# A recurrent-attention and Fourier-mixing kernel: another pairing and order of the last token tiles, and another list of steps

## The chip, the core and the metric

One core of a Trainium2 chip runs the whole program. The metric is device time in microseconds (us), the median of several executions. Engines: PE multiplies matrices, PEld is its weight load, DVE is the vector engine, ACT the scalar engine, POOL GpSimd, SP the sync engine, which here only issues DMAs. Each engine works through its own instructions in program order and waits on semaphores for the others.

## The reference

```python
# q, k, v, f_logit: (4 batches, 8 heads, 768 tokens, 48)
f = 1 / (1 + exp(-f_logit))
for t in range(768):
    state = f[t][:, None] * state + outer(k[t], v[t])
    y[t] = q[t] @ state
x = y, heads side by side                       # (4, 768, 384)
u = x + real(fft(fft(x, axis=1), axis=2))
un = (u - mean(u)) / sqrt(var(u) + 1e-6)        # over the 384 channels
out = u + maximum(un @ w_ch1, 0) @ w_ch2        # 384 -> 1536 -> 384
```

## The kernel before, in words

**Order by hand.** The program is written out by a list of words, ORDER (lines 27 to 48, 720 words). Each word runs one step of some generator, and every step appends its instructions to the queues of the engines it uses. So the list is the order on every engine, DMA issues on SP and POOL included. The tile framework adds the waits. The words:

- A number u (0 to 15): the next step of attention unit u, two heads of one batch (`attention`, `outputs`, `fold`). Batch b has the units 4b to 4b+3. The steps are: ACT Exp and Ln (L372, L373); DVE scan (L379, L380); ACT three Exp (L383 to L387); DVE two products (L391, L392); PE scores (L400); DVE masked copy (L404); PE first values and more scores, ACT copy `ao` (L559 to L579); PE other values and the state update `ds` (L559, L599); DVE state scan (L607); PE values from the state, ACT five copies (L616 to L629); PE transposes, ACT two copies (L636 to L641); DVE fold (L663 to L669); for the last two units of a batch one more fold (L678 to L687).
- K u: PE transposes the keys of unit u (L538) and ACT copies them to `kT` (L540), which `ds` reads.
- L u names: SP loads f, k, q or v of unit u (L206 to L213). r, R: SP fetches one or three of 24 raw 384 KB weight blocks into three buffers (L310). C: a block is turned into fp32 by ACT (L281), DVE (L283, L284) and POOL (L285); the first 12 blocks are `w1`, the other 12 `w2`.
- F b: a step of the Fourier stage of batch b: four of `z` (PE L725, ACT copies), then three of `mix` (PE L744, DVE sums, `moments`, `deviation`). H b: a step of `turns` (line 786), which normalizes a tile of 128 tokens (`moments`, `deviation`) or transposes it (`turn`, L780 to L784) for the products.
- P b: a step of `projected` (line 855): tiles of 128 tokens go in three pairs. For batch 0 the first layer is L872, and its first pair takes the plain second product `po` (L881, L885). For batches 1 to 3 the first layer is `hidden`, 15 steps a pair (L841 to L852), from sums of blocks. The second layer is seven products of quarter blocks, each 12 matmul records (L895), into two PSUM tiles `fx` (halves X, Y) and `fz` (halves V, Z); DVE makes sums for them (L902 to L913) and adds the results to the four half-rows c1, c2, d1, d2 of the pair's tiles c and d (L906 to L929), which `store` writes out.
- W, B: DVE makes the sums of weight blocks (L358 to L361, L813, L815). V, c: near the end weight blocks are read again and their smallest magnitude taken (L336, L344). M: `judge` (line 940) makes of these a flag, which every engine loads (line 1005) before a branch (line 1007) around a repair path that is not taken here.
- I, Z: POOL fills constants (`start`, with `bound`, which the first scan and the fillers read; `zeros`). D: eight filler matmuls on `bound` (L192). i, T, S: tables and the identity.

**Stores** (line 689). Tiles 1, 2, 3 and 5 go out by an indirect DMA from POOL, since their rows lie in another order; tiles 0 and 4 by plain DMAs from SP, tile 4 in three pieces (1, 15 and 112 rows); tile 0 of the last batch from ACT. All write the one output tensor, and the framework lets a store after an indirect one wait for its landing.

**The end.** The last batch's pairs are LAST_PAIRS = ((2, 5), (1, 4), (3, 0)). In the last pair tile 3 is c and tile 0 is d; product 7 into X ends it, and one DVE instruction (L929) adds X to both halves of tile 0's rows.

Of the kernel before, what the change touches and what calls it, by code (L numbers as in the profile page):

```python
# [10 lines left out]
ALU = mybir.AluOpType  # L11

C = 128
# [14 lines left out]
    "I L0f D L1f 0 D 0 1 L2f D D D D D L0q L0k D L1k 2 Z 0 D 1 i D D L1q L3q 0 0 0 L0v L3fk D 1 r 1 L2q D "  # L28
    "D L1v L2k 2 0 1 K0 3 0 0 D r 3 r D 2 0 1 1 2 C K1 L2v 1 2 1 C 3 2 C 1 K2 3 L4fk 4 2 r 1 2 L5fk D 4 5 "
    "L3v 1 3 2 D D T C 2 3 0 L4qv K3 5 3 0 2 3 D 3 2 3 S 2 3 D 3 L6fk 6 R 3 4 F0 5 F0 4 L5qv F0 C F0 5 "  # L30
    "L6qv K4 C r C 4 4 r F0 5 4 H0 H0 r C 4 H0 4 C L7fk r F0 r 7 F0 6 4 P0 C L7qv K5 P0 P0 r C r 5 C P0 r "
    "7 P0 5 6 4 6 P0 C C P0 5 K6 5 L8fk r C P0 7 7 P0 5 6 r P0 C 8 P0 r 6 r C P0 6 7 C K7 H0 C r 7 P0 r 6 "
    "C r 6 5 P0 C 6 H0 C P0 B 7 r C 6 r C 7 H0 L9fk L8qv P0 8 P0 P0 9 9 7 9 L9qv 6 P0 P0 P0 P0 9 7 9 K9 "
    "H0 P0 8 9 P0 P0 7 5 P0 P0 B P0 P0 8 7 B 9 8 4 9 H0 B W P0 P0 P0 9 P0 6 P0 P0 L11fk B P0 11 P0 P0 P0 "
    "P0 B B P0 11 9 8 K8 7 P0 P0 P0 11 8 F1 F1 F1 P0 P0 B L11qv F1 B P0 8 11 8 F1 11 8 L10fk P0 H1 B 10 B "
    "K11 P0 P0 P0 P0 L10qv 10 B 10 P0 10 P0 P0 10 H1 11 P0 P0 10 B B P0 B P0 H1 B P0 10 K10 P1 P1 P1 P1 "
    "P1 P1 P1 P1 L12fk P1 P1 P1 P1 P1 P1 F1 P1 F1 10 8 12 10 P1 8 12 10 12 9 P1 P1 P1 P1 L12qv 12 11 9 12 "
    "P1 H1 P1 H1 P1 12 11 K12 H1 H1 11 11 H1 L13fk P1 P1 P1 L13qv P1 P1 P1 P1 P1 P1 13 P1 P1 P1 P1 P1 13 "
    "P1 P1 12 10 P1 P1 13 13 12 10 12 11 P1 P1 P1 11 10 P1 L14fk 14 12 P1 K13 P1 11 F2 F2 P1 P1 14 P1 P1 "
    "L14qv P1 F2 P1 P1 14 P1 P1 P1 P1 P1 P1 14 F2 13 F2 P1 13 F2 P1 13 F2 P1 13 14 L15fk H2 15 13 14 13 "  # L40
    "K14 P1 15 L15qv 15 P1 P1 P1 14 15 H2 P1 H2 14 H2 P1 P2 14 P2 P2 P2 P2 P2 P2 P2 P2 P2 P2 P2 P2 P2 P2 "
    "13 14 15 K15 H2 H2 15 15 14 P2 V 15 H2 14 15 13 P2 14 c V 15 12 12 P2 P2 15 P2 15 V P2 P2 15 P2 F3 "
    "F3 F3 P2 H2 c V P2 P2 P2 V V P2 P2 P2 P2 P2 P2 P2 c P2 c c F3 P2 V F3 V F3 V c P2 P2 F3 P2 P2 P2 P2 "
    "P2 P2 H3 P2 H3 P2 V P2 P2 H3 P2 c P2 c c P2 P2 V P2 P2 P2 P2 P2 P2 P2 V P2 P2 P2 c c P2 c V V c V P2 "
    "V P2 P2 V P2 P2 H3 P3 c H3 P3 P3 P3 P3 P3 P3 P3 P3 P3 P3 P3 P3 c P2 P3 P3 H3 c P3 P3 P3 V P3 V P3 V "
    "c P3 P3 H3 P3 P3 H3 P3 c V P3 P3 P3 P3 P3 P3 P3 P3 V P3 P3 P3 P3 c P3 c P3 P3 P3 P3 P3 P3 P3 P3 P3 "
    "P3 V P3 c c P3 P3 P3 P3 P3 P3 c V P3 c P3 P3 P3 P3 P3 M P3 P3 P3 P3 P3 P3 P3 P3"
# [32 lines left out]
LAST_PAIRS = ((2, 5), (1, 4), (3, 0))  # L80
# [3 lines left out]
def kernel(  # L84
# [13 lines left out]
    nc = tc.nc  # L98
    B, HP, _, D, _, S = qkf.shape
# [589 lines left out]
    def store(b, c, rows):  # L689
# [7 lines left out]
        for i, j, o in {0: [(0, C, 0)], 4: [(0, 1, 3 * QS), (1, 16, HS + 1), (16, C, HS + 16)]}[c]:  # L697
            queue = nc.scalar if (b, c) == (B - 1, 0) else nc.sync
            queue.dma_start(out=out[b, o:o + j - i], in_=rows[i:j])
# [3 lines left out]
    def fnet(b, x):  # L703
# [52 lines left out]
        H1 = QD + 1  # L756
# [98 lines left out]
    def projected(b, x, again=False):  # L855
# [5 lines left out]
        for j, (c, d) in enumerate(PAIRS if b < B - 1 else LAST_PAIRS):  # L861
            if again:
                for _ in range((3, 3, 2)[j] if b < B - 1 else (3, 2, 3)[j]):
                    next(behind[b], None)
# [49 lines left out]
            yield  # L914
# [181 lines left out]
```

## Time and profile before

| | us |
|---|---|
| median of three runs (527.76 to 528.81) | 528.33 |
| the profiled execution | 527.43 |
| its span, first to last instruction | 525.7 |
| PE busy in it | 494.9 |
| DVE busy | 378.6 |
| ACT busy | 216.8 |

A profile is of one execution. The span lies within its time, with 1.75 us around it. Instructions are named by line, engine, operation and tiles (out<-in); "idle before" is the time in which the engine had nothing to run just ahead of one, and the name after it what ended that. A matmul's end is modelled, so PE can look full where it is only nearly so. PEclk is the clock that the chip granted to PE, in tenths.

The costliest groups (busy us, mean ns, idle before):

```profile
L850 DVE TENSOR_TENSOR h<-h,ub 128x512 f32<-128x512 f32 x81 | 55.6, 688 | 38.9 <-PE ub L841 27.2
L872 PE MATMUL up<-unT,w 128*128 128x256 f32 x216 | 50.0, 382 | 0.0
L841 PE MATMUL ub<-wide,w 128*128 128x128 f32 x360 | 45.2, 277 | 2.1 <-DVE wide L815 2.1
L895 PE MATMUL fx<-block,h 128*128 128x192 f32 x264 | 46.8, 327 | 0.0
L379 DVE TENSOR_TENSOR_SCAN W<-g,bound 112x768 f32<-112x768 f32 x12 | 21.2, 1766 | 8.7 <-ACT g L373 8.7
```

### The profile page before, as it was taken

What the parts mean: (1) busy time and instruction counts of PE and PEld (TensorE: products, weight loads), DVE (VectorE), ACT (ScalarE), POOL (GpSimd) and SP (SyncE); (2) the same over time, 40 slices, a digit from 0 to 9 for tenths busy, and PEclk for the clock granted to TensorE, in tenths of its full rate; (3) what the DMA queues carried; (4) which work ended last, traced back from release to release, by engine and by line L of the source; (5) the groups of instructions that cost most, each with busy time, mean ns of one, the idle gap of its engine ahead of it and who ended that gap; (6) DMA issues with size and microseconds to landing.
All of it is one profiled execution on the core that took longest, in us unless ns stands there. A gap on an engine that the chain in (4) does not pass through costs nothing.

```text
span 525.7 us, 13813 instructions
## 1 busy us (share of the span) xinstructions
PE 494.9 (94%) x5854; PEld 452.8 (86%) x5854; DVE 378.6 (72%) x746; ACT 216.8 (41%) x520; POOL 61.3 (12%) x85
## 2 busy tenths in 40 slices
PE   6788699989999999999999999999999999999994
PEld 5676478756898889999999999998999999999994
DVE  4669999868986378588688696679586665565571
ACT  7484658753423351452543524341431404131220
POOL 3047034541002000000001000000001000010000
PEclk9879799999999999999999999999999999999998
DMA  8979476672002110222112012122140330410201
GB/s 222 277 192 268 98 198 187 184 215 85 28 28 85 54 56 28 57 55 86 54 56 84 1 55 73 46 62 68 53 122 15 107 135 1 136 61 1 92 2 36
DMA packets 20505, 48.15 MB, mean 92 GB/s; under 512 B 3409, under 2 KB 6034, under 8 KB 20434
## 3 DMA queue, kind: packets, MB, share of 16 engines
q1 hardware_dynamic: 19186, 43.43, 29.3%
q0 software_dynamic: 1104, 3.54, 1.8%
q8 instruction: 48, 0.79, 0.6%
q14 instruction: 23, 0.19, 0.1%
q10 hardware_dynamic: 144, 0.20, 0.1%
HBM read 42.44 MB, written 4.72 MB: 90 GB/s over the span
## 4 chain that ended last, share of the span: by engine, by line
PE 80%; DVE 9%; DMA 4%; issue 2%; ACT 2%; SPq 0%; POOL 0%; DVEq 0%; POOLq 0%; ACTq 0%
PE ub L841 23%; PE fx L895 16%; PE fz L895 12%; PE up L872 6%; PE z L725 4%; PE mix L744 3%; PE y L559 3%; PE po L881 2%; PE sc L400 2%; PE y L616 2%; DMA raw<-in_w_ch_dram 2%; PE pt L783 2%; PE ds L599 1%; PE st L538 1%; DVE W L379 1%
## 5 line engine op out<-in xcount | busy, mean ns | idle before, releaser
L850 DVE TENSOR_TENSOR h<-h,ub 128x512 f32<-128x512 f32 x81 | 55.6, 688 | 38.9 <-PE ub L841 27.2
L692 POOL DMA_INDIRECT out_dram<-x,place x16 | 17.7, 1107 | 383.7 <-DVE x L925 254.0
L848 ACT ACTIVATE h<-ub 128x512 f32<-128x512 f32 x54 | 32.0, 593 | 45.0 <-PE ub L841 45.0
L872 PE MATMUL up<-unT,w 128*128 128x256 f32 x216 | 50.0, 382 | 0.0
L841 PE MATMUL ub<-wide,w 128*128 128x128 f32 x360 | 45.2, 277 | 2.1 <-DVE wide L815 2.1
L895 PE MATMUL fx<-block,h 128*128 128x192 f32 x264 | 46.8, 327 | 0.0
L895 PE MATMUL fx<-w,h 128*128 128x192 f32 x264 | 45.6, 327 | 0.0
L872 PEld LDWEIGHTS up<-unT,w 128*128 128x128 f32 x216 | 39.8, 190 | 6.2 <-ACT h L874 0.9
L841 PEld LDWEIGHTS ub<-wide,w 128*128 128x128 f32 x360 | 42.4, 192 | 3.1 <-PE fx L895 1.2
L895 PEld LDWEIGHTS fx<-block,h 128*128 128x128 f32 x264 | 43.3, 190 | 0.4 <-DVE x L922 0.2
L852 ACT ACTIVATE h<-h 128x512 f32<-128x512 f32 x45 | 28.3, 630 | 36.9 <-DVE h L850 36.8
L895 PEld LDWEIGHTS fx<-w,h 128*128 128x128 f32 x264 | 42.8, 190 | 0.4 <-issue 0.2
L841 PE MATMUL ub<-unT,w 128*128 128x128 f32 x288 | 36.8, 275 | 0.0
L285 POOL TENSOR_TENSOR w<-w,raw 128x384 uint32<-128x384 uint32 x24 | 28.1, 1173 | 71.6 <-ACT raw L281 42.8
L841 PEld LDWEIGHTS ub<-unT,w 128*128 128x128 f32 x288 | 34.5, 192 | 0.1
L784 ACT COPY unT<-pt 128x384 f32<-128x384 f32 x24 | 11.4, 485 | 48.5 <-PE pt L783 48.5
L841 PE MATMUL ub<-unT,wide 128*128 128x128 f32 x216 | 29.1, 278 | 0.0
L841 PE MATMUL ub<-wide 128*128 128x128 f32 x216 | 28.6, 275 | 0.4 <-DVE wide L815 0.4
L379 DVE TENSOR_TENSOR_SCAN W<-g,bound 112x768 f32<-112x768 f32 x12 | 21.2, 1766 | 8.7 <-ACT g L373 8.7
L874 ACT ACTIVATE h<-up 128x256 f32<-128x256 f32 x36 | 13.8, 386 | 31.7 <-PE up L872 31.4
L841 PEld LDWEIGHTS ub<-unT,wide 128*128 128x128 f32 x216 | 26.4, 192 | 0.5
L841 PEld LDWEIGHTS ub<-wide 128*128 128x128 f32 x216 | 26.3, 192 | 0.5 <-PE ub L841 0.5
(189 smaller groups left out, 1001.6 us busy)
## 6 DMA issues: line engine op xcount, KB each, us to landing
raw<-in_w_ch_dram SPq DMA_DIRECT2D x24, 384.0 KB, 5.3
v<-in_v_dram SPq DMA_DIRECT2D x16, 288.0 KB
k<-in_w_ch_dram SPq DMA_DIRECT2D x12, 384.0 KB
g<-in_w_ch_dram SPq DMA_DIRECT2D x12, 384.0 KB, 3.5
k<-in_qkf_dram SPq DMA_DIRECT2D x14, 288.0 KB, 5.9
g<-in_qkf_dram SPq DMA_DIRECT2D x12, 288.0 KB, 5.6
q<-in_qkf_dram SPq DMA_DIRECT2D x12, 288.0 KB, 4.9
wide<-in_qkf_dram SPq DMA_DIRECT2D x10, 288.0 KB, 5.2
```

Of the source, the lines that this page charges most:

```text
L285: nc.gpsimd.tensor_tensor(bits, bits, lo, ALU.add)
L379: nc.vector.tensor_tensor_scan(W, g, bound[:R], 0.0, ALU.add, ALU.min)
L559: nc.tensor.matmul(y[FILL[g], c // 3, c % 3 * C + t.start:c % 3 * C + t.stop], lhsT=vals[rows, o:o + (64 if g == 0 else D)], rhs=weights, ...
L692: nc.gpsimd.indirect_dma_start(out=out.rearrange("b s d -> (b s) d"), out_offset=bass.IndirectOffsetOnAxis(ap=place[:, b, i:i + 1], axis=0 ...
L725: nc.tensor.matmul(z[:, cols], lhsT=src[:, j, lo:hi], rhs=tab[:, t, T % 2, cols], start=(i == 0), stop=(i == len(parts) - 1), skip_group_c ...
L744: nc.tensor.matmul(mix[:, o], lhsT=zz[:rows_of[T], T, PLACES[c]], rhs=cd[:rows_of[T], T, :NQ - odd], start=(i == 0), stop=(i == 1))
L841: nc.tensor.matmul(chains[chain][:, m * 128:(m + 1) * 128], lhsT=block(w)[:, m * 128:(m + 1) * 128], rhs=tokens(a), start=(new and m == 0) ...
L848: nc.scalar.activation(out, got, kind, scale=1.0 if how == "=+" else -1.0)
L850: nc.vector.tensor_tensor(out, out, got, ALU.add if how == "+" else ALU.subtract)
L852: nc.scalar.activation(out, out, AF.Relu)
L872: nc.tensor.matmul(pp[:, :256], lhsT=w1[:, kt, m * 128:(m + 1) * 128], rhs=unT[:, kt], start=(kt == 0), stop=(kt == 2))
L895: nc.tensor.matmul(out, lhsT=h[:, m], rhs=blocks[i][:, m], start=(start and m == 0), stop=(m == H - 1), skip_group_check=True)
```

## The change

Three things change. The list has the same 720 words in another order. LAST_PAIRS becomes ((2, 5), (1, 3), (0, 4)), and `turns` follows it. For the pair (0, 4) the products come in the order 1, 2, 4, 6, 5, 7, 3, so that the last one adds to c2 alone, the second half of tile 0's rows; tile 4 is complete one product earlier and is stored then; tile 0 goes out in two halves of 192 columns, both from SP.

```diff
@@ -25,26 +25,26 @@
 
 
 ORDER = (
-    "I L0f D L1f 0 D 0 1 L2f D D D D D L0q L0k D L1k 2 Z 0 D 1 i D D L1q L3q 0 0 0 L0v L3fk D 1 r 1 L2q D "
-    "D L1v L2k 2 0 1 K0 3 0 0 D r 3 r D 2 0 1 1 2 C K1 L2v 1 2 1 C 3 2 C 1 K2 3 L4fk 4 2 r 1 2 L5fk D 4 5 "
-    "L3v 1 3 2 D D T C 2 3 0 L4qv K3 5 3 0 2 3 D 3 2 3 S 2 3 D 3 L6fk 6 R 3 4 F0 5 F0 4 L5qv F0 C F0 5 "
-    "L6qv K4 C r C 4 4 r F0 5 4 H0 H0 r C 4 H0 4 C L7fk r F0 r 7 F0 6 4 P0 C L7qv K5 P0 P0 r C r 5 C P0 r "
-    "7 P0 5 6 4 6 P0 C C P0 5 K6 5 L8fk r C P0 7 7 P0 5 6 r P0 C 8 P0 r 6 r C P0 6 7 C K7 H0 C r 7 P0 r 6 "
-    "C r 6 5 P0 C 6 H0 C P0 B 7 r C 6 r C 7 H0 L9fk L8qv P0 8 P0 P0 9 9 7 9 L9qv 6 P0 P0 P0 P0 9 7 9 K9 "
-    "H0 P0 8 9 P0 P0 7 5 P0 P0 B P0 P0 8 7 B 9 8 4 9 H0 B W P0 P0 P0 9 P0 6 P0 P0 L11fk B P0 11 P0 P0 P0 "
-    "P0 B B P0 11 9 8 K8 7 P0 P0 P0 11 8 F1 F1 F1 P0 P0 B L11qv F1 B P0 8 11 8 F1 11 8 L10fk P0 H1 B 10 B "
-    "K11 P0 P0 P0 P0 L10qv 10 B 10 P0 10 P0 P0 10 H1 11 P0 P0 10 B B P0 B P0 H1 B P0 10 K10 P1 P1 P1 P1 "
-    "P1 P1 P1 P1 L12fk P1 P1 P1 P1 P1 P1 F1 P1 F1 10 8 12 10 P1 8 12 10 12 9 P1 P1 P1 P1 L12qv 12 11 9 12 "
-    "P1 H1 P1 H1 P1 12 11 K12 H1 H1 11 11 H1 L13fk P1 P1 P1 L13qv P1 P1 P1 P1 P1 P1 13 P1 P1 P1 P1 P1 13 "
-    "P1 P1 12 10 P1 P1 13 13 12 10 12 11 P1 P1 P1 11 10 P1 L14fk 14 12 P1 K13 P1 11 F2 F2 P1 P1 14 P1 P1 "
-    "L14qv P1 F2 P1 P1 14 P1 P1 P1 P1 P1 P1 14 F2 13 F2 P1 13 F2 P1 13 F2 P1 13 14 L15fk H2 15 13 14 13 "
-    "K14 P1 15 L15qv 15 P1 P1 P1 14 15 H2 P1 H2 14 H2 P1 P2 14 P2 P2 P2 P2 P2 P2 P2 P2 P2 P2 P2 P2 P2 P2 "
-    "13 14 15 K15 H2 H2 15 15 14 P2 V 15 H2 14 15 13 P2 14 c V 15 12 12 P2 P2 15 P2 15 V P2 P2 15 P2 F3 "
-    "F3 F3 P2 H2 c V P2 P2 P2 V V P2 P2 P2 P2 P2 P2 P2 c P2 c c F3 P2 V F3 V F3 V c P2 P2 F3 P2 P2 P2 P2 "
-    "P2 P2 H3 P2 H3 P2 V P2 P2 H3 P2 c P2 c c P2 P2 V P2 P2 P2 P2 P2 P2 P2 V P2 P2 P2 c c P2 c V V c V P2 "
-    "V P2 P2 V P2 P2 H3 P3 c H3 P3 P3 P3 P3 P3 P3 P3 P3 P3 P3 P3 P3 c P2 P3 P3 H3 c P3 P3 P3 V P3 V P3 V "
-    "c P3 P3 H3 P3 P3 H3 P3 c V P3 P3 P3 P3 P3 P3 P3 P3 V P3 P3 P3 P3 c P3 c P3 P3 P3 P3 P3 P3 P3 P3 P3 "
-    "P3 V P3 c c P3 P3 P3 P3 P3 P3 c V P3 c P3 P3 P3 P3 P3 M P3 P3 P3 P3 P3 P3 P3 P3"
+    "L0f Z I 0 L0q L2q D D L1f L0k D 0 D 0 i D 1 L2f 2 0 D D D L0v 0 L1k K0 D 0 0 D L1q 0 1 D r 1 L3fk D "
+    "D D L1v 2 0 L2k 1 D r r D 1 2 1 3 3 0 C K1 1 2 0 C 1 L3q 2 1 3 C L2v 2 r K2 L4fk 3 L3v L5fk 1 2 1 D "
+    "T 2 0 4 3 D C S 1 2 5 3 D 2 3 2 4 K3 3 D L5qv L4qv 5 4 3 2 3 L6fk 3 2 3 5 R 3 F0 F0 4 6 F0 L6qv F0 C "
+    "C 4 C 5 4 F0 r 5 K4 D 4 H0 r 4 r H0 C H0 4 C r L7fk F0 6 4 P0 C P0 6 5 P0 7 C F0 4 P0 r K5 r C L7qv "
+    "P0 P0 r r 5 6 C 6 5 r 7 C 5 P0 r 7 P0 C P0 5 r 7 K6 C P0 6 C P0 r r 6 7 7 C C 6 6 r 5 P0 P0 r C 6 r "
+    "C K7 H0 r P0 C 7 L9fk 6 H0 L8fk P0 L8qv C B 7 C H0 B 7 B 9 9 B 8 P0 8 9 P0 P0 L9qv P0 6 8 P0 P0 P0 "
+    "P0 9 P0 P0 8 7 B 9 K9 P0 P0 5 P0 B 6 P0 P0 B P0 7 W P0 9 B H0 9 8 9 B H0 7 P0 L11fk P0 11 P0 P0 P0 "
+    "P0 P0 P0 4 11 9 P0 P0 P0 P0 P0 9 B P0 P0 P0 P0 7 L11qv P0 8 11 F1 P0 8 K8 F1 F1 11 F1 L10fk 8 8 10 "
+    "F1 P0 8 11 H1 L10qv B 10 F1 P0 B P0 B P0 11 P0 P0 10 B 10 H1 P0 10 K10 P0 B 10 H1 10 K11 L12fk P1 P1 "
+    "P1 P1 P1 P1 P1 B P1 P1 P1 P1 P0 P1 P1 P1 F1 P1 P1 H1 10 9 12 10 P1 P1 12 10 9 8 P1 P1 P1 L12qv 12 11 "
+    "12 12 8 11 P1 L13fk 12 11 H1 10 H1 P1 11 H1 H1 P1 P1 P1 P1 P1 P1 P1 P1 P1 P1 P1 P1 P1 P1 10 P1 P1 12 "
+    "K12 10 P1 12 L13qv 11 P1 L14fk 12 11 P1 13 13 12 P1 P1 11 P1 14 13 P1 F2 P1 14 F2 P1 P1 P1 P1 P1 P1 "
+    "P1 P1 P1 P1 P1 14 P1 13 F2 P1 L14qv 14 P1 F2 13 13 F2 13 K13 F2 14 13 H2 F2 13 14 H2 P1 L15fk P1 P1 "
+    "15 15 13 K14 P1 P1 L15qv P1 14 P1 H2 14 H2 H2 P2 14 P2 P2 15 P2 P2 P1 P2 P2 P2 15 V P2 P2 P2 P2 P2 "
+    "P2 P2 13 14 15 H2 H2 15 K15 15 13 12 15 14 P2 15 14 15 P2 P2 V c 12 P2 15 P2 c V 14 P2 15 P2 H2 P2 "
+    "P2 P2 15 c F3 F3 F3 P2 V V P2 P2 P2 c V c P2 V P2 c P2 P2 V P2 F3 c P2 P2 V F3 F3 P2 F3 H3 P2 P2 P2 "
+    "P2 P2 P2 P2 P2 H3 P2 V P2 P2 V H3 P2 P2 c P2 P2 V P2 c c P2 P2 P2 V P2 P2 P2 P2 P2 P2 P2 c P2 P2 V "
+    "P2 H3 V P2 P2 H3 P3 H3 c P3 P3 c P3 P3 c P3 P3 P3 P3 c V P3 V P2 P3 P3 P3 c P3 P3 P3 P3 P3 V V P3 P3 "
+    "P3 P3 V H3 P3 P3 P3 H3 P3 c P3 P3 P3 P3 c P3 P3 P3 P3 P3 V P3 P3 P3 P3 P3 P3 P3 P3 c P3 P3 P3 P3 P3 "
+    "V P3 P3 c P3 V P3 c P3 c P3 P3 V c c P3 P3 P3 P3 P3 P3 M P3 P3 P3 P3 P3 P3 P3 P3"
 )
 
 
@@ -77,7 +77,7 @@
 FLIP = 1
 
 PAIRS = ((0, 3), (2, 5), (1, 4))
-LAST_PAIRS = ((2, 5), (1, 4), (3, 0))
+LAST_PAIRS = ((2, 5), (1, 3), (0, 4))
 
 
 @with_exitstack
@@ -695,8 +695,7 @@
                 in_=rows, in_offset=None)
             return
         for i, j, o in {0: [(0, C, 0)], 4: [(0, 1, 3 * QS), (1, 16, HS + 1), (16, C, HS + 16)]}[c]:
-            queue = nc.scalar if (b, c) == (B - 1, 0) else nc.sync
-            queue.dma_start(out=out[b, o:o + j - i], in_=rows[i:j])
+            nc.sync.dma_start(out=out[b, o:o + j - i], in_=rows[i:j])
 
     behind, turned_of = {}, {}
 
@@ -785,7 +784,7 @@
 
         def turns():
 
-            for step in ((0, [3], 3, [4, 5], 2, 5, 1, 4) if b < B - 1 else ([4, 5], 2, 5, 1, 4, [3], 3, 0)):
+            for step in ((0, [3], 3, [4, 5], 2, 5, 1, 4) if b < B - 1 else ([4, 5], 2, 5, [3], 1, 3, 0, 4)):
                 if isinstance(step, list):
                     for c in step:
                         moments(c)
@@ -860,7 +859,7 @@
         tt = nc.vector.tensor_tensor
         for j, (c, d) in enumerate(PAIRS if b < B - 1 else LAST_PAIRS):
             if again:
-                for _ in range((3, 3, 2)[j] if b < B - 1 else (3, 2, 3)[j]):
+                for _ in range((3, 3, 2)[j]):
                     next(behind[b], None)
             unT = turned_of[b][j].rearrange("p k t n -> p k (t n)")
             h = ph1.tile([128, NF, 2, 128], F32, tag="h1", name=f"h1_{b}_{j}")
@@ -912,6 +911,26 @@
             tt(c1, Y, c1, ALU.add)
             tt(h12, h12, h11, ALU.subtract)
             yield
+            both = x[:, d].rearrange("p (a n) -> p a n", a=2)
+            if (b, c) == (B - 1, 0):
+                nc.sync.dma_start(out=out[b, :C, :HD], in_=c1)
+                product(6, X, h11)
+                tt(d1, V, d1, ALU.add)
+                yield
+                product(5, Z, s1)
+                tt(c2, X, c2, ALU.add)
+                yield
+                product(7, X, h21)
+                tt(d2, Z, d2, ALU.add)
+                yield
+                product(3, Z, h12)
+                tt(both, X.unsqueeze(1).to_broadcast([128, 2, HD]), both, ALU.add)
+                store(b, d, x[:, d])
+                yield
+                tt(c2, Z, c2, ALU.add)
+                nc.sync.dma_start(out=out[b, :C, HD:], in_=c2)
+                yield
+                continue
             product(5, Z, s1)
             tt(d1, V, d1, ALU.add)
             yield
@@ -925,7 +944,6 @@
             tt(c2, Z, c2, ALU.add)
             store(b, c, x[:, c])
             yield
-            both = x[:, d].rearrange("p (a n) -> p a n", a=2)
             tt(both, X.unsqueeze(1).to_broadcast([128, 2, HD]), both, ALU.add)
             store(b, d, x[:, d])
             yield
```

## The prediction

> **What bounds the kernel now.** I read the page's totals and its slices first, then stretches of 25 us.
>
> ```profile
> span 525.7 us, 13813 instructions
> PE 494.9 (94%) x5854; PEld 452.8 (86%) x5854; DVE 378.6 (72%) x746; ACT 216.8 (41%) x520; POOL 61.3 (12%) x85
> PEclk9879799999999999999999999999999999999998
> ```
>
> PE at 94% looks like the bound of everything, but the slices differ. The table of stretches (PE, PEld, DVE, ACT, POOL busy, then granted clock, DMA share, GB/s) shows where:
>
> ```profile
> 0.00:25.00 25.00, 16.90 (x352) 15.61 (x352) 13.67 (x15) 15.07 (x24) 4.78 (x29) 0.93 0.96 244
> 25.00:50.00 25.00, 21.62 (x566) 18.17 (x566) 20.48 (x36) 15.71 (x40) 12.65 (x17) 0.86 0.86 223
> 50.00:75.00 25.00, 18.23 (x305) 14.35 (x306) 23.35 (x51) 15.25 (x43) 7.05 (x8) 0.86 0.60 162
> 75.00:100.00 25.00, 25.00 (x347) 20.88 (x348) 24.22 (x38) 19.79 (x50) 10.71 (x8) 1.00 0.68 186
> 100.00:125.00 25.00, 23.09 (x337) 15.54 (x328) 18.32 (x32) 13.19 (x31) 8.39 (x8) 1.00 0.64 188
> 125.00:150.00 25.00, 25.00 (x335) 21.64 (x334) 22.32 (x42) 11.24 (x29) 1.51 (x1) 1.00 0.12 37
> ```
>
> From 25 to 100 us DVE is full and PE is not; from 125 on PE is full. So the head of the list is a DVE stage, the rest a PE stage. The DVE's waits up to 60 us and the chain around 110 us say how the first ends:
>
> ```profile
> DVE stt L607 <- PE ds L599: 7.0, 2, 3.8
> DVE W L379 <- ACT g L373: 6.3, 1, 6.3
> DVE at L404 <- PE sc L400: 1.2, 1, 1.2
> ```
>
> ```profile
> 109.37 5.48 DMA raw<-in_w_ch_dram
> 114.85 0.02 issue
> 114.87 0.37 DVE w L283
> ```
>
> DVE loses 6.34 us to the first load and its Exp and Ln, 1.20 to unit 0's scores and 7.0 to the state scans of units 0 and 1 (3.25 at 18.4, 3.77 at 28.0), 14.8 with a gap of 0.2. From 31.8 to 102 it has no gap over 0.3 us. Then the last raw weight blocks pace it (a block is fetched when the third one before it has left POOL), until block 24 is converted and PE runs on at 116.8. After that PE's waits over 0.3 us sum to 3.7 us in 400.
>
> Tail: the last product ends at 518.85, and then
>
> ```profile
> 518.88 0.56 DVE L929 TENSOR_TENSOR x<-fx,x 128x384 f32<-128x384 f32 x1 [1.59 <-PE fx L895]
> 520.42 0.38 ACTq L699 DMA_DIRECT2D out_dram<-x  x1
> ```
>
> ACT issues 0.98 us after DVE has finished: its wait (504.22 to 520.38) ends with the landing of tile 3's indirect store (last at 520.35). The store lands at 523.60, SP then walks its closing waits from 523.61 to 524.87, and the span ends at 525.66: 6.81 us after PE.
>
> **The last pair.** It has the same seven products (1.95 us each) in another order, so PE is unchanged. Product 6 comes 1.95 us earlier: it needs h11, which L907 finished at 510.35, where PE would load for it at 510.72, so 0.37 us of cover. Product 3 is last and only a 128x192 add follows: 0.36 (rows L922, L925) in place of 0.56. Tile 3's indirect store is now in the middle pair, some 28 us earlier, so nothing is left to wait for. Tile 4's three stores come into this pair on SP: L699 issued such three from 490.60 to 491.70, 1.1 us, and they fall under product 3 (1.95 us from its predecessor's end, less 0.6 for the add). With that cover gone, the last store is up to 1.1 later. Where they stood before, two rereads (L336, issued 491.74 and 492.21) were queued behind them on SP; those are freed, and the flag they feed was ready at 505.5, 13 us early, so that is worth nothing. Counting from PE's end: add done 0.40, SP issues 0.45 to 0.82, landing about 2.6 (L699's median is 2.0 from issue). That would save 2 us. But SP also has its flag load and its branch behind that store. Before, they ran at 505.51 to 506.42 (0.91), and the next SP event came at 509.09, 2.67 later, hidden under products. Now they lie on the path: 0.82 + 0.05 + 0.91 + 2.67 = 4.45, and 0.18 for two waits that SP had passed before: 4.63 against 4.76. **Tail: -0.1**; bounds -2.0 (the 2.67 hidden after all) and +1.1 (PE's own branch took 3.79).
>
> [...]
>
> LAST_PAIRS and the turns move one moments step (0.73 DVE, 0.5 ACT) from before the third pair's turns to before the second's, under some 330 us of PE-bound time already past: 0, at worst the 0.7 itself. The counts (3, 2, 3) belong to the branch that is not taken.
>
> **The head of the list.** Every word occurs as often as before (720 words), so only order counts. Up to the first F0 both lists hold the same DVE work: four units, four weight blocks, the scans of units 4 and 5, 45.0 us by the means of the rows (per unit scan 1.94, L391 and L392 1.91, L404 1.03, L607 0.75, fold 2.46; L283 and L284 1.15 per block; 4.2 for the two later folds); up to block 24 both hold 95.5. So DVE's lead is its idle time alone, and I replay the new order with row durations:
> - Z ahead of I puts 2.54 us of POOL (3.29 to 5.83 before) ahead of `bound`: ready at 4.4, not 1.9. Fillers start later; the first scan, at 6.34, keeps 1.9 of cover.
> - DVE: scan 0 from 6.34 to 8.3, as before. ACT now does unit 0's Exp (0.84) next, ahead of units 1 and 2: DVE waits 0.9 and multiplies from 9.2 to 11.1 (before: to 12.4).
> - PE scores to 12.2 (DVE waits 1.1), copy to 13.2, scan 1 to 15.1, scan 2 to 17.05.
> - ACT: unit 0 to 10.5, Exp and Ln of unit 1 to 12.3, of unit 2 to 14.2, kT (K0, moved up) to 14.85, ao to 15.35. PE's values and ds (0.85 + 0.8) end at 17.0: the state scan waits for nothing, where it waited 3.25.
> - State scan to 17.8, unit 1's products to 19.7. PE has six fillers (0.67 each) after ds, to 21.0, and scores to 22.0: DVE waits 2.3.
> - Then scan 3, C, unit 2's products and C lead to unit 1's state scan at 29.2; its ds is there at 27.4. Cover 1.8 where 3.77 was lost.
>
> Idle 6.34 + 0.9 + 1.1 + 2.3 = 10.6 against 14.8, so **4.2 us** of lead. PE had two waits put to "issue" here, 1.15 at 17.4 and 2.26 at 22.7, which I cannot place in the new order; I take off half of the smaller: **-3.6**. Bounds: -4.5 and, if the two together fall on DVE's path, -0.8.
>
> Does the lead reach PE? Take, for each PE step that needs a DVE step, the DVE work ahead of and with the one less the PE work ahead of the other. Its largest value is 8.7 before (unit 5's copy, 69.8 against 61.1) and 8.6 after (unit 6's products, 72.8 against 64.2); the largest sets how late PE is for a given DVE. So PE follows by the same 3.6. The weight blocks: 12, 15, 18, 21 and 24 were begun at 83.9, 92.5, 99.6, 106.7 and 114.9; their places in DVE work are the same within 2 us, and L8fk no longer stands between the fetches (it was issued at 87.9 to 90.6, ahead of a fetch at 91.5). Three blocks in 7.5 us from a start 3.6 earlier: block 24 at 111.3, -3.6 again. Its adds then find po done, so the 2.58 us that DVE waited at L885 may shrink; that is DVE's, not the path's.
>
> **The rest of the list** reorders PE steps whose sum is the same. Unit 12's scores stand straight after their DVE products (1.07 us of PE work between them before), while units 8, 9 and 11 gain such cover. Bounds: all 3.7 us of PE's waits gone, or as much again; nearest to the equal sum of covers, I take +0.2.
>
> Sum on the profiled run (527.43, that is the span and 1.75 around it): -0.1 - 3.6 + 0.2 = -3.5, so 523.9. The median of the three is 0.90 above it: **524.8**, own range 522.5 to 527.0.
>
> **Rivals.**
> 1. *More.* PE's waits at issue fall where DVE does not care (-0.6 more), the branch's fetch overlaps (-1.0) and the block waits shrink by half (-1.7): 521.5. For it: 102 to 117 is paced by fetches, and L8fk leaves them. Against: the fetch cycle of 7.5 us is buffers, not traffic.
> 2. *One state scan waits again.* Unit 3's stands right behind K3 and its values; by the replay its ds comes 0.4 us before DVE wants it. One wait of the old size (3.25 to 3.77) gives the lead back: 524.8 + 3.5 = 528.3, no change.
> 3. *Slower: unit 0's v is late.* q0 and q2 now go ahead of f1 and f2, with DMA engines 96% busy. Ahead of and with v0 stand 2.56 MB (six loads of about 0.34, ident, v): at the 222 GB/s of the first slice it lands at 12.3, at the 98 of the worst slice near 27. PE waits for it in order, the state scan with it, and DVE stands behind the scan. Later than 13.2 it costs what it is late; from 17.4 the lead is gone; from 18.5 the kernel is measurably slower; at 19.5 it is +2.1 net: 530.4. For it: no landing of v is listed. Against: k and q land in 5 to 6 us, and v0 is issued three microseconds earlier than it was.
>
> **Chances.** The forecast 0.50, rival 1 0.16, rival 2 0.14, rival 3 0.20. A difference of 0.2% (1.06 us) is about what this measurement tells from none. Faster: 0.50 (less 0.015), 0.16, and a quarter of rival 2: 0.68; slower: rival 3 and a little of rival 2: 0.21; same: 0.11. The range holds rival 1's near half and rival 3 up to 530: 521.0 to 530.0.
>
> **What would show it.** DVE's first waits: 0.9, 1.1 and 2.3 in place of 1.2, 3.25 and 3.77; the first z of batch 0 near 54 (57.6 before); block 24 begun near 111.3; PE's last end near 515.4; SP's last store 0.45 after it and SP's first closing wait 3.6 after that store's issue has ended. Wrong would be: a state scan that waits 3 us again, v0 landing after 13.2, or PE's waits after 125 us growing past 4 us.

## The result

| | before | after |
|---|---|---|
| median of 20 runs, us | 528.32 (527.42 to 531.83) | 525.92 (523.41 to 529.41) |
| ratio after to before | | 0.9957, 95% interval 0.9940 to 0.9974 |
| the profiled execution | 527.43 | 527.98 |
| its span | 525.7 | 526.3 |

The change saves 2.4 us in the median. The execution that was profiled with the result is one of the long ones of its kernel: it is longer than the profiled one of before, though the median is shorter. So the changed kernel was profiled a second time (called "the second execution" below: 524.12 us, span 522.3). The two traces of one program, side by side, show what an execution can do to the head of the list.

From the page of the first execution: span, busy engines, and the granted clock in 40 slices.

```profile
span 526.3 us, 13807 instructions
PE 494.9 (94%) x5854; PEld 453.4 (86%) x5854; DVE 378.3 (72%) x746; ACT 218.4 (42%) x520; POOL 58.8 (11%) x85
PEclk9789699999999999999999999999999999999998
```

Its stretches (PE, PEld, DVE, ACT, POOL busy, then granted clock, DMA share, GB/s):

```profile
0.00:25.00 25.00, 16.14 (x301) 14.90 (x301) 11.13 (x12) 15.28 (x24) 4.80 (x29) 0.86 0.96 249
25.00:50.00 25.00, 19.93 (x558) 16.76 (x561) 23.31 (x37) 15.33 (x40) 10.07 (x11) 0.86 0.66 169
50.00:75.00 25.00, 18.93 (x341) 14.26 (x333) 21.19 (x48) 13.98 (x40) 6.26 (x13) 0.80 0.67 181
100.00:125.00 25.00, 23.74 (x372) 16.60 (x371) 21.80 (x35) 16.27 (x35) 9.53 (x9) 1.00 0.69 196
```

PE's busy time is 494.9 in both kernels, whose matmuls (5854) are the same. In the first 25 us DVE did less than before (11.13 against 13.67), at a granted clock of 0.86 against 0.93; between 100 and 125 it did more (21.80 against 18.32), because its waits for the raw blocks have shrunk (from 98 to 125 us: 1.7 in place of 3.7) and its wait of 2.6 for `po` is gone. The same stretches of the second execution:

```profile
0.00:25.00 25.00, 16.38 (x366) 14.89 (x367) 13.50 (x14) 15.39 (x24) 4.82 (x29) 1.00 0.94 242
100.00:125.00 25.00, 24.65 (x238) 16.58 (x239) 23.13 (x41) 16.17 (x34) 7.52 (x7) 1.00 0.72 204
```

DVE's waits up to 60 us (total, times, longest), first execution and then the second:

```profile
DVE W L379 <- ACT g L373: 6.5, 1, 6.5
DVE at L404 <- PE sc L400: 4.3, 2, 3.1
DVE stt L607 <- PE ds L599: 4.2, 2, 2.8
```

```profile
DVE at L404 <- PE sc L400: 2.4, 2, 1.2
DVE stt L607 <- PE ds L599: 4.0, 3, 1.5
```

The state scans (L607) waited 7.0 us before; they still wait 4.2 and 4.0. The scores (L404) waited 1.2 before and now 4.3 or 2.4, because the second unit's scores have six fillers ahead of them.

The chain around 110 us, first execution and then the second:

```profile
112.18 4.41 DMA raw<-in_w_ch_dram
116.58 0.02 issue
116.61 0.37 DVE w L283
```

```profile
108.34 3.60 DMA raw<-in_w_ch_dram
111.94 0.02 issue
111.97 0.95 DVE w L283
```

Block 24 is converted at 116.6 and 112.0 (114.9 before). PE's last matmul ends at 519.43 and 515.32 (518.84 before). The distance between these two marks is 402.8, 403.4 and 404.0: **what happens ahead of block 24 arrives at the end nearly undiminished, and what lies behind it differs by 1.1 us between these three traces.** Between the two executions of the changed kernel block 24 differs by 4.6 us and the rest by 0.5, so this spread is made in the first 115 us. In the fourteen traces of this study that distance lies between 402.8 and 405.5.

The tail, from the timeline of the first execution (start, duration, instruction):

```profile
517.52 0.56 DVE L927 TENSOR_TENSOR x<-fx,x 128x384 f32<-128x384 f32 x1 [1.59 <-PE fx L894]
518.15 1.33 SPq L698 DMA_DIRECT2D out_dram<-x  x3
519.47 0.36 DVE L930 TENSOR_TENSOR x<-fz,x 128x192 f32<-128x192 f32 x1 [1.39 <-PE fz L894]
519.86 0.36 SPq L931 DMA_DIRECT2D out_dram<-x  x1
```

The last add is 0.36 long and the store is issued 0.43 after PE's end, as the change intends; ACT's wait for an indirect store is gone. But the span still ends 6.82 us after PE's last matmul (6.99 in the second execution), where it was 6.84. SP's own waits at the end say why:

```profile
SPq L1025 <- SPq L1025: 2.5, 1, 2.5
```

After its last store SP runs its flag load (520.27) and a branch that ends at 521.20; its next event comes at 523.69, 2.49 us later (2.54 in the second execution). This line is those 2.49 us: it names nothing but SP itself that they wait for. The DMA's instruction queue (q14 on the page) starts a packet of 8 KB in them at 522.10, 0.90 us after the branch's end and 1.59 ahead of that event.

### The profile page after: what moved, and what is told of

Same layout as the page of the kernel before. It is cut to its first block, busy times and chain, and to the rows that moved or that the text cites. A ratio compares the mean times of both kernels' runs of the same rounds, so it can differ in the third digit from the quotient of the medians.

```text
span 526.3 us, 13807 instructions
## 1 busy us (share of the span) xinstructions
PE 494.9 (94%) x5854; PEld 453.4 (86%) x5854; DVE 378.3 (72%) x746; ACT 218.4 (42%) x520; POOL 58.8 (11%) x85
## 4 chain that ended last, share of the span: by engine, by line
PE 87%; DVE 6%; issue 2%; ACT 2%; DMA 1%; POOL 0%; SPq 0%; DVEq 0%; ACTq 0%
PE ub L840 23%; PE fx L894 16%; PE fz L894 11%; PE up L871 9%; PE z L724 5%; PE y L559 4%; PE mix L743 3%; PE y L616 2%; PE sc L400 2%; PE ds L599 2%; PE po L880 2%; PE yt L636 2%; PE pt L782 1%; PE st L538 1%; PE y L192 1%
## 5 line engine op out<-in xcount | busy, mean ns | idle before, releaser
L849 DVE TENSOR_TENSOR h<-h,ub 128x512 f32<-128x512 f32 x81 | 55.2, 687 | 33.5 <-PE ub L840 24.5
L692 POOL DMA_INDIRECT out_dram<-x,place x16 | 16.4, 1024 | 357.6 <-DVE x L944 224.3
L285 POOL TENSOR_TENSOR w<-w,raw 128x384 uint32<-128x384 uint32 x24 | 29.4, 1228 | 72.3 <-DVE w L284 39.1
```

Of the source, the lines that this page charges most:

```text
L285: nc.gpsimd.tensor_tensor(bits, bits, lo, ALU.add)
L692: nc.gpsimd.indirect_dma_start(out=out.rearrange("b s d -> (b s) d"), out_offset=bass.IndirectOffsetOnAxis(ap=place[:, b, i:i + 1], axis=0 ...
L849: nc.vector.tensor_tensor(out, out, got, ALU.add if how == "+" else ALU.subtract)
```

## The experiments

Ratios are to runs of the kernel before on the same chip, medians of 11 to 12 runs (7 in experiment 7) with their 95% intervals. "The changed kernel" is that of the result.

**1. The head of the list alone.** The kernel before, with the new list up to the sixteenth P0 (about 115 us of the program), the old list behind it, and the old last pair.

```diff
-    "I L0f D L1f 0 D 0 1 L2f D D D D D L0q L0k D L1k 2 Z 0 D 1 i D D L1q L3q 0 0 0 L0v L3fk D 1 r 1 L2q D "
+    "L0f Z I 0 L0q L2q D D L1f L0k D 0 D 0 i D 1 L2f 2 0 D D D L0v 0 L1k K0 D 0 0 D L1q 0 1 D r 1 L3fk D "
...
```

> The kernel before with the new list up to the second product of batch 0's first tile, and the old list behind it; pairs and stores are the old ones. Theory H (the gain is made in the head of the list, where DVE waits less): 0.9955 to 0.997 of the kernel before, 526.0 to 526.7 us. Theory R (it is made behind the head, in the middle of the list or the last pair): 528.3 us, ratio 1.000 within 0.001.

Measured: 526.23 against 528.76, ratio 0.9968 [0.9944, 0.9993]. In its trace block 24 is begun at 111.5 (114.9 before), PE ends at 516.36, and the span ends 7.07 later. The head alone brings 1.7 us by the ratio (0.4 to 3.0 by its interval), most of what the whole change brings. The profiled execution is the shortest of its twelve.

**2. The last pair alone.** The changed kernel with the whole old list.

```diff
-    "L0f Z I 0 L0q L2q D D L1f L0k D 0 D 0 i D 1 L2f 2 0 D D D L0v 0 L1k K0 D 0 0 D L1q 0 1 D r 1 L3fk D "
+    "I L0f D L1f 0 D 0 1 L2f D D D D D L0q L0k D L1k 2 Z 0 D 1 i D D L1q L3q 0 0 0 L0v L3fk D 1 r 1 L2q D "
...
```

> The changed kernel with the whole old list: new pairs, new product order, halves of tile 0 from SP. Theory H: 528.3 us, ratio 1.000 within 0.001, since SP's flag load and branch eat what the earlier store saves: 6.8 us from PE's end to the span's end, as before. Theory T (the earlier store is worth the 1.0 us that ACT waited for the landing, and the smaller add 0.2): 527.1 us, ratio 0.9977.

Measured: 530.30 against 528.76, ratio 1.0041 [1.0014, 1.0069]: slower. The tail took 7.14 us after PE's end, 0.3 more than before. Both theories miss this. Its trace also has a gap of PE that the changed kernel does not have, 0.85 us at 447 us (PE's waits from 440 to 455):

```profile
PE pt L782 <- DVE un L779: 0.8, 1, 0.8
```

The new pairs move a turn (moments and H3) to another tile, and the old places of H3 in the list do not suit it. So, by this one trace, the old list and the new pairs do not fit together, and the two parts of the change are not independent. The span of this trace is 2.3 us longer than that of before: 0.5 of it lies ahead of block 24, 1.5 between block 24 and PE's end (with the 0.85 of this gap) and 0.3 in the tail. The other 0.7 behind block 24 are not placed.

**3. The list and the pairs, without the special product order.** The changed kernel without the branch for tile 0 of the last batch: the old order of products, tile 0 whole, tile 4 last with three stores from SP.

```diff
-            if (b, c) == (B - 1, 0):
-                nc.sync.dma_start(out=out[b, :C, :HD], in_=c1)
...
-                nc.sync.dma_start(out=out[b, :C, HD:], in_=c2)
-                yield
-                continue
```

> The changed kernel without its own code for the last pair: new list and pairs, but the products in the old order, tile 0 stored whole and earlier, tile 4 last, with three stores from SP behind the 0.56 us add. Theory H: the changed kernel plus 1.1 us, 527.0 us, for SP then reaches its branch 1.1 us later (0.56 + three issues of 1.1 to 1.3 us against 0.36 + 0.36), 7.9 us from PE's end to the span's. Theory T (the landing of the last store sets the end): the changed kernel plus 0.2 to 1.3 us of landing and no shift of SP's branch. Theory R: as the changed kernel within 0.3 us.

Measured: 526.38 against 528.76, ratio 0.9955 [0.9933, 0.9978], not to be told from the whole change (0.9957). Its tail is 7.53 after PE's end, less than the 7.9 of theory H. The special order is worth the 0.5 to 0.7 us by which the tails differ (6.99 and 6.82 with it); with the spread of the head that does not show in a median.

**4. The last stores from ACT.** If SP's branch is what eats the tail's gain, SP should reach it early and another engine should do the last stores.

```diff
-            nc.sync.dma_start(out=out[b, o:o + j - i], in_=rows[i:j])
+            queue = nc.scalar if (b, c) == (B - 1, 4) else nc.sync
+            queue.dma_start(out=out[b, o:o + j - i], in_=rows[i:j])
...
-                nc.sync.dma_start(out=out[b, :C, HD:], in_=c2)
+                nc.scalar.dma_start(out=out[b, :C, HD:], in_=c2)
```

> The changed kernel with tile 4's three stores and tile 0's second half issued by ACT; SP's last store is tile 0's first half, 8 us before PE's end, so SP's branch and its fetch (2.5 us) are done early. If SP's branch is on the path (my theory): SP's closing waits begin when the last store has landed, 2.7 us after PE's end instead of 4.26, ACT's own branch is over at 4.3 and its closing ends there, and the span ends 5.2 us after PE's end instead of 6.82: 1.6 us less than the changed kernel, 524.3 us. If the landing and the closing chain set the end alone (rival): no more than 0.3 us less, 525.6 to 525.9 us.

> The kernel in which ACT issues the last pair's stores, a second time, in more rounds. My theory (SP's branch and its fetch of 2.5 us are what ate the tail's gain, so that storing from ACT gives 1.5 us whatever the head does): the span ends 5.1 to 5.4 us after PE's last matmul (6.8 to 7.1 in the changed kernel), and the ratio to the kernel before lies about 1.5/528 = 0.003 under the changed kernel's 0.9957, so 0.991 to 0.995. The rival (the first 0.9922 was a lucky mix of heads, and the tail is worth nothing): 0.9957 to 0.998, whatever the profile's tail shows.

Measured: 524.57 against 528.76, ratio 0.9922 [0.9900, 0.9944]; and a second time 524.48 against 528.54, ratio 0.9925 [0.9901, 0.9950]. The span ends 5.29 and 5.30 us after PE's last matmul. The timeline of the first of these profiles, and then SP's waits in it:

```profile
518.51 1.34 ACTq L699 DMA_DIRECT2D out_dram<-x  x3
519.87 0.36 DVE L931 TENSOR_TENSOR x<-fz,x 128x192 f32<-128x192 f32 x1 [1.39 <-PE fz L895]
520.26 0.36 ACTq L932 DMA_DIRECT2D out_dram<-x  x1
```

```profile
SPq L1110 <- DVEq L1026: 0.8, 1, 0.8
SPq L1110 <- ACTq L1026: 0.3, 1, 0.3
```

SP now passes its branch under the products and its closing waits stand for the others: the last store's landing, then DVE's event (its branch ended at 520.58, its next event is at 523.75, 3.17 later) and ACT's (521.27 to 524.17, 2.90). ACT's branch is over no sooner than SP's was: 4.33 us after PE's end against 4.26. What is saved is SP's closing work behind the branch. In the changed kernel SP walks through some twenty closing events from 523.69 to 525.13; here it has walked through most of them by 522.99, under the branches of DVE and ACT. So the 1.5 us (6.82 less 5.29) are what SP no longer does after everybody else. This version is the fastest of all by its median, twice.

**5. The changed kernel again.**

> The changed kernel once more, on the same chip as the three below, for its spread and a second profile. 0.994 to 0.9975 of the kernel before. Theory F (PE runs out of fetched instructions at its 449th and every 256 after it, in a head whose DMA engines are full): the wait at the 449th stands again in unit 0's values, 1.5 to 2.5 us, whatever the clock. Theory G (the granted clock alone makes the spread): it need not.

Measured: 526.31 against 528.14, ratio 0.9972 [0.9946, 0.9997]. This is the second execution shown above. The wait that theory F expects at the 449th is there again, 1.93 us long.

**6. Without the early fillers.** Seven of the ten D words ahead of unit 0's state update are taken out (a D is a filler: 8 small matmuls on `bound` whose result nobody reads).

```diff
-    "L0f Z I 0 L0q L2q D D L1f L0k D 0 D 0 i D 1 L2f 2 0 D D D L0v 0 L1k K0 D 0 0 D L1q 0 1 D r 1 L3fk D "
...
+    "L0f Z I 0 L0q L2q D D L1f L0k D 0 0 i 1 L2f 2 0 L0v 0 L1k K0 0 0 L1q 0 1 D r 1 L3fk D D D L1v 2 0 "
...
```

> The changed kernel without seven of the ten filler groups ahead of unit 0's state update: 112 PE instructions fewer, so its 449th is now a filler behind that update. Theory F: the state scan of unit 0 waits 0.3 to 0.8 us instead of 2.8, and the time falls by 1 to 2 us against the changed kernel (0.992 to 0.994). Theory G (fillers hold the clock): PE stands idle for some 5 us ahead of unit 0's scores, the granted clock up to 50 us falls under 0.86, and the time is equal or up to 2 us more (0.996 to 1.000).

Measured: 529.68 against 528.14, ratio 1.0035 [1.0008, 1.0061], some 3.4 us worse than the changed kernel on the same chip (experiment 5). PE's timeline around unit 0's scores, without the early fillers and then in the changed kernel:

```profile
11.43 1.65 PE L400 MATMUL sc<-q,g 48*64 48x64 f32 x48 [4.10 <-DVE g L392]
14.30 0.92 PE L559 MATMUL y<-at,v 64*48 64x64 f32 x24
```

```profile
11.48 1.03 PE L400 MATMUL sc<-q,g 48*64 48x64 f32 x48 [1.80 <-DVE g L392]
13.72 0.57 PE L559 MATMUL y<-at,v 64*48 64x64 f32 x24
```

The same matmuls take 1.6 times as long after 4.10 us of rest as after 1.80, and DVE's wait for these scores grows from 1.20 to 1.82. The granted clock in the stretches of the profile is 1.00 in both from 5 to 17 us, so the profile's clock column does not show this slowness; the durations do. The ratio is near that of another pair: where the granted clock does read 0.5, the state update `ds` takes 1.43 in place of 0.85, 1.7 times as long. What made these matmuls slow is not shown, and the length of the rest alone does not decide it: in experiment 8 the scores took 1.03 after 4.23 us of rest, and what ran from 12.8 to 16.2, at a granted clock of 0.5, was slow.

Both theories miss the time. The count of theory F holds: number 449 now lies in a filler behind `ds`, and PE does not stop there. But unit 0's state scan still waits 1.46 us, with `ds` at 1.43, and the scans of units 1 and 3 wait 2.65 and 2.82.

**7. Without the late fillers.** The six D words between unit 0's state update and unit 1's scores are taken out.

```diff
-    "... K0 D 0 0 D L1q 0 1 D r 1 L3fk D D D L1v 2 0 L2k 1 D r r D 1 2 ..."
+    "... K0 D 0 0 D L1q 0 1 r 1 L3fk L1v 2 0 L2k 1 r r 1 2 ..."
```

> The changed kernel without the six filler groups between unit 0's state update and unit 1's scores. The masked copy of unit 1 waited 3.1 us, for scores that stood behind 4.9 us of fillers. If DVE is what bounds the head (my theory): that wait falls to about 1.2 us, and the time by 1 to 2 us against the changed kernel (0.992 to 0.994). Theory G: the clock falls, values and scores take longer, and the time is equal or up to 2 us more (0.996 to 1.000).

Measured: 531.38 against 528.14, ratio 1.0066 [1.0036, 1.0096], 5.1 us worse than the changed kernel (experiment 5), more than either theory allowed. The unit 1 scores do come sooner (DVE waits 1.20 for them), but the state scans of units 1 and 3 then wait 2.44 and 4.14. The granted clock, in stretches as above:

```profile
20.00:40.00 20.00, 16.31 (x402) 13.81 (x406) 15.79 (x27) 12.30 (x30) 5.02 (x7) 0.74 0.91 243
40.00:60.00 20.00, 11.83 (x245) 9.90 (x245) 14.74 (x30) 11.08 (x27) 7.37 (x13) 0.74 0.81 219
```

In the two executions of the changed kernel it is 0.76 and 0.83 from 20 to 40 us, and 0.84 in both from 40 to 60: lower here in the second stretch, and in the first only against the second execution. A filler that stands in the path of the next scores costs some 0.5 us of PE (2.85 for six); taking these six away cost more than that.

**8. Z at its old place on POOL.**

```diff
-    "L0f Z I 0 L0q L2q D D L1f L0k D ...
+    "L0f I 0 L0q L2q D D L1f Z L0k D ...
```

> The changed kernel with POOL's constants in the old order (Z behind I, ahead of L0k): fillers start at 1.9 us instead of 4.6 and end 2.7 us earlier, so that PE stands idle for 4.5 us instead of 2.0 ahead of unit 0's scores. Theory G: the granted clock of the first 25 us falls and the time rises by 0.5 to 2 us (0.997 to 0.9995). My theory (only DVE's waits count, and none is ended by the fillers or by bound here): no change within 0.5 us (0.995 to 0.997).

Measured: 526.71 against 528.14, ratio 0.9965 [0.9938, 0.9992], not to be told from the changed kernel (0.9972), nor, by its interval, from theory G's range. Whether the fillers start at 1.92 or 4.6 us makes no difference that shows: DVE's wait for ACT ahead of the first scan is 6.7 here and 6.5 and 6.3 in the changed kernel.

**9. More fillers.** If fillers pay by themselves, through the granted clock as theory G has it, more of them should help. Five D ahead of the first F0 in the version of experiment 4 and in the kernel before, where PE rests some 4 us ahead of the first z; and then two D more in each of three gaps.

```diff
-    ... 3 2 3 5 R 3 F0 F0 4 6 F0 ...
+    ... 3 2 3 5 R 3 D D D D D F0 F0 4 6 F0 ...
```

> The kernel with the last stores on ACT (0.992 of the kernel before) with five filler groups more, ahead of the first z product of batch 0, where PE stood idle for 4.6 us and then ran the z products at half clock (8.2 us for what takes some 5.3). Theory G (the half clock of the head is on the path): the z products at full clock, 2 to 3 us earlier end, 0.987 to 0.990. Theory D (DVE alone sets the head; z is hidden behind its work): 0.992 within 0.001.

> The kernel before with the same five filler groups ahead of its first z product (idle 4.1 us, then half clock). Theory G: 0.995 to 0.997, as much gain as the new list made. Theory D: 1.000 within 0.001.

```diff
-    ... L3v L5fk 1 2 1 D T ... 2 3 2 4 K3 ... L6fk 3 2 3 5 R ...
+    ... L3v L5fk 1 D D 2 1 D T ... 2 D D 3 2 4 K3 ... L6fk D D 3 2 3 5 R ...
```

> As z_fill, with two filler groups more in each of three gaps of 1.4 us in which PE waits for ACT's five copies (ahead of the first values of units 2 and 3 and of unit 3's transposes). Theory G: half-clock stretches between 25 and 50 us go too, 0.985 to 0.988. Rival: the fillers take 1.3 to 2.6 us each and stand ahead of work that DVE waits for, so 1 to 2 us more than z_fill.

Measured: 525.59 (0.9955 [0.9934, 0.9976]), 530.22 (1.0031 [1.0011, 1.0051]) and 528.57 (1.0003 [0.9978, 1.0027]), all against 528.43. All three are slower than any of the theories had it. With five fillers the first z, once begun, runs quicker (1.51 us for its first six matmuls in place of 2.85) and the z products end 1.1 to 1.3 us sooner than in the profile of before and in the first of experiment 4 (1.0 later than in its second), but block 24 is later all the same (118.9 against 115.9 and 114.6 in experiment 4, 116.0 against 114.9 in the kernel before). The third has the best mean clock of all traces (0.989) and is 4 us slower than the version of experiment 4. Its stretch from 20 to 40 us and its waits from 98 to 125 us:

```profile
20.00:40.00 20.00, 15.88 (x468) 13.63 (x466) 17.16 (x29) 13.24 (x32) 4.84 (x7) 1.00 0.98 249
```

```profile
DVE w L283 <- DMA raw<-in_w_ch_dram: 5.2, 3, 2.5
```

So the theory that the mean clock alone decides falls: seven of the third version's runs had a mean clock of 0.991 to 0.996 and took 525.4 to 529.0 us. Where its time goes is shown only in part: unit 3's state scan waits 4.66, in a stretch (44.6 to 51.5) where the granted clock is 0.5, and the blocks are late. The fillers that were there already are worth 3 to 5 us; those added here cost 1 to 4.

## Why the prediction came out as it did

The forecast was 524.8, faster, and 525.92 was measured: right in its sign, with a gain of 2.4 us, a third less than the 3.5 of the sum. The mechanism held only in part. The tail came out as worked out; the lead was made ahead of block 24, as forecast, but mostly not by the waits that the replay took away. That the median came so near is partly luck.

**The tail** was worked out as -0.1 and measured as 0.0 and +0.15: 6.82 and 6.99 us against 6.84. The step that made it small, SP's flag load and branch behind the store with a cost taken from another place of the trace (2.67), held: 2.49, with SP's closing wait at 4.53 after PE's end where 4.63 was worked out. Experiment 4 shows that SP's closing was on the path, since moving the stores to ACT brings 1.5 us twice. Rival 1's "the branch's fetch overlaps" does not happen in the changed kernel: the 8 KB packet of instructions starts 0.90 us after SP's branch has ended, and 1.59 more pass before SP's next event.

**The rest of the list** was put at +0.2. Block 24 to PE's end is 1.1 and 0.6 us shorter than before, and PE's waits over 0.3 us after 125 us sum to 2.8 in place of 3.7. That is inside the bounds given, on the good side. That the turns and pairs cost nothing is true only with the new list: with the old one, experiment 2's trace has 0.85 us of PE lost to them.

**The head** is the term that was mis-sized. It was put at -3.6; the head alone measured -1.7 (-0.4 to -3.0). One reading under it was wrong: from 75 to 100 us PE is full too (25.00 of 25 in the prediction's own table), so DVE alone sets the pace only up to about 75 us. The replay was right in much of its detail: fillers from 4.6 (4.4 worked out), DVE's next waits 0.97 (0.9) and 1.20 (1.1). It failed at the sentence "the state scan waits for nothing", with ds ready at 17.0. The scan waited 2.82 and 1.55. PE's timeline there, first execution and then the second:

```profile
18.33 0.48 PE L559 MATMUL y<-at,v 64*48 64x64 f32 x7 [2.25 <-issue]
18.74 1.43 PE L599 MATMUL ds<-v,kT 128*64 128x48 f32 x20
20.11 4.93 PE L192 MATMUL y<-bound 128*128 128x128 bf16 x48
24.97 0.93 PE L400 MATMUL sc<-q,g 48*64 48x64 f32 x48
```

```profile
17.61 0.33 PE L559 MATMUL y<-at,v 64*48 64x64 f32 x7 [1.71 <-issue]
17.88 0.85 PE L599 MATMUL ds<-v,kT 128*64 128x48 f32 x20
18.65 2.85 PE L192 MATMUL y<-bound 128*128 128x128 bf16 x48
21.53 1.05 PE L400 MATMUL sc<-q,g 48*64 48x64 f32 x48
```

In the middle of unit 0's 24 values PE stops, after 17 of them, and "issue" ends it: it waits for no other engine and no landing that the profile names. Take the 1.71 away and ds ends at 17.0, exactly where the replay had it. These are the waits that the prediction could not place and charged with half of the smaller, 0.6; in the new order one of them stands right ahead of ds. They are not tied to a step of the list but to a count. With PE's records of the trace numbered from 0 (weight loads, matmuls, semaphore steps), they stand at number 449 and at whole multiples of 256 behind it: before at 449, 705 and 1217; in the first execution at 449 and 1473, in the second at 449 and 705; in the head alone at 449, 705, 961 and 1217. (The 4 us that PE rests ahead of the first z, and five other rests of 0.4 to 3.0 us in the fourteen traces, are also put to issue, but stand at other counts; what they wait for is not shown.)

These stops go with the instruction queue of the DMA (q8 on the page: 48 packets, 0.79 MB, before and after). It moves seven or eight packets of 16 KB in the first 62 us of every trace, one for each of these counts in their order. In the fourteen traces PE stopped for over 0.3 us at 37 of these counts, and in all 37 it went on 2.5 to 2.9 us after the start of the packet (2.86, 2.73 and 2.62 before, 2.60 and 2.78 in the first execution). Where it did not stop, the packet had mostly started earlier (3.66 and 4.39 us ahead at 1473 and 1729 before).

In the order before, number 449 lay in the second unit's scores. In the new order it lies in unit 0's values. For the ten traces of the new order in which it does, the time from the PE record before number 449 to it, and what DVE then waited for ds:

| trace | gap at number 449, us | state scan's wait, us | ds took, us |
|---|---|---|---|
| experiment 1 | 1.08 | 0.69 | 0.85 |
| experiment 5 (second execution) | 1.93 | 1.55 | 0.85 |
| experiment 4, first profile | 2.35 | 1.97 | 0.85 |
| experiment 4, second profile | 2.28 | 2.48 | 1.44 |
| experiment 9, five fillers | 2.90 | 3.12 | 1.43 |
| the result (first execution) | 2.47 | 2.82 | 1.43 |
| experiment 3 | 1.93 | 1.54 | 0.85 |
| experiment 7 | 1.45 | 1.07 | 0.85 |
| experiment 9, all fillers | 1.51 | 1.12 | 0.85 |
| experiment 8 | 0.93 | 1.88 | 0.85 |

In the rows with ds at 0.85, but for the last, the wait is the gap less 0.38: ds had 0.38 us of cover, and all of the gap beyond it went to DVE. Where the granted clock was 0.5 just then, the 0.58 by which ds is longer comes on top (and in the first execution 0.15 by which the seven values left are longer: 2.47 - 0.38 + 0.58 + 0.15 = 2.82). In experiment 8 the granted clock was 0.5 from 12.8 to 16.2, PE began unit 0's values a microsecond later (14.73), and the wait is 1.3 more than the gap explains. That accounts for unit 0's wait in nine of ten traces; that the time would fall by it if the stop lay elsewhere is not shown, since in experiment 6, which moved it, PE was slow there as well.

The fillers behind ds are the second piece. They were put at 0.67 each, 4.0 in all, and DVE's wait at 2.3. They take 2.85 at full clock and 4.93 at half: a wait of 1.20 or 3.08 (1.92 to 2.62 in three traces where the clock was halved for a part of them), so the estimate was between two states, neither of which it named.

With these, DVE's idle time up to the first z was not 10.6 but 16.1 in the first execution (6.48 + 0.97 + 1.20 + 2.82 + 3.08 + 1.35, and a gap of 0.2) and 14.0 in the second (14.8 before): of the 4.2 us of lead, 0.8 in the better of the two. The first z came at 59.5 and 57.0 (57.6 before, near 54 forecast). In the second execution more of the lead appears later: from the first z to block 24 it takes 55.0 us against 57.3, where DVE's waits for raw blocks have shrunk from 3.7 to 0.9 us and its wait of 2.6 for po has gone. Rival 1 named that shrinking as worth 1.7. Of the 3.5 us by which PE's end is earlier in the second execution, 0.7 are there at the first z, 2.3 come between it and block 24, and 0.6 behind it. That the shrunken waits are the cause of the 2.3 is not shown: in the first execution they shrank as well (to 1.7), and this stretch is only 0.2 shorter (57.1). So the good execution ends nearly where the forecast put it (block 24 at 112.0 against 111.3, PE's end at 515.32 against 515.4), but for other reasons than those given, and the median lies between it and the first.

**The rivals.** Unit 0's v was not late: PE began the values at 13.72, straight behind its own transposes and a filler, and no DMA ended a wait there. The wait of unit 3's state scan, rival 2, is real but comes and goes. From experiment 4's first profile and from the second execution:

```profile
51.97 0.76 DVE L607 TENSOR_TENSOR_SCAN stt<-ds,te 112x288 f32<-112x288 f32 x1 [4.47 <-PE ds L599]
```

```profile
48.92 0.76 DVE L607 TENSOR_TENSOR_SCAN stt<-ds,te 112x288 f32<-112x288 f32 x1 [1.27 <-PE ds L599]
```

The granted clock tells them apart. In the eleven traces of the new order, this wait is 1.24 to 1.35 in the five in which the granted clock was 0.5 for less than 1 us of the 8 us ahead of the scan (the two executions of the changed kernel, experiments 1 and 3, experiment 4's second profile). It is 2.82 in experiment 6, with 3.4 us of it, and 4.06 to 4.66 in the five with 6.5 to 7.6 us of it (experiment 4's first profile, experiments 7 and 8, and the two of experiment 9 that start from the new order). In the two executions shown, PE's work from the scan before it to the end of this `ds` takes 9.1 and 5.9 us, and DVE's own work beside it 5.5 in both. So up to 3 us of DVE's time in the head hang on where the stretches of half clock fall; how much of an execution's length is the clock's and how much the fetches' stays open, for both stand in the same 60 us, and no run here held one of them still.

## What to carry to other kernels

When a gain at the end of a kernel is counted, follow the engine that does the last store to its last instruction, not only the store to its landing. Here SP also closes the program behind its branch, and giving the last stores to another engine let SP do that beforehand. When a list is reordered in a stage of many short instructions like this head, count the instructions of the engine: here PE's waits for its instruction packets (0.4 to 2.9 us) stayed at number 449 and at whole multiples of 256 behind it, and landed on whatever then stood there. A gain of two or three microseconds by replay is no more certain than those waits, and than the place of the stretches at half clock. And profile such a kernel twice before explaining a difference of 0.5%.

## What the runs showed of the hardware

- **PE's waits for its instruction packets show as "issue".** In the first 45 us of the fourteen traces PE stopped for 0.4 to 2.9 us at record number 449 or multiples of 256 behind it. It went on 2.5 to 2.9 us after the start of a 16 KB packet of the instruction queue, which itself takes 0.9 to 1.4 us (2.1 once). The DMA engines were 94 to 96% busy in the first 25 us of each; whether PE would stop with idle DMA engines no run here shows.
- **Behind the branch at the end an engine's next event comes 2.4 to 3.3 us later**, in the fourteen traces, where it has no store to wait for: 2.44 to 2.67 on SP, 2.39 to 2.96 on ACT, 2.85 to 3.29 on DVE, 2.50 to 3.14 on POOL. In the traces of before and of the first execution a packet of 8 KB of the instruction queue starts 0.9 to 1.1 us after the end of each of these eight branches and 1.6 to 1.9 ahead of the event; it is this that is called the branch's fetch here.
- **The granted clock differs between executions of one program.** In the first 70 us it changes between 0.5 and 1.0, and the stretches at 0.5 last 3.41 or 6.83 us before and 6.83 or 10.24 in the first execution: from 17.7 to 24.5, 34.7 to 41.6 and 55.2 to 65.5 in the first execution, from 26.2 to 29.6, 36.4 to 39.8 and 53.5 to 60.3 in the second. Of the twenty runs of the changed kernel, those with a mean clock of 0.973 to 0.974 took 527.98 to 529.41 us and those with 0.985 to 0.990 took 523.41 to 525.70. This goes together; that the clock is the cause of the whole time is not shown, and experiment 9 has a kernel with a better clock and a longer time. One wait is seen to go with it: unit 3's state scan waits 1.2 to 1.4 us where the clock ahead of it is nearly whole, and 4.1 to 4.7 where it is halved.
